# RWKV-7 recurrence and a cosine MoE on one core: the recurrence in units of 64 steps of two batches

## Chip, cores and metric

One core of a Trainium2 chip runs the whole program in one launch. The metric is the device time of that core in microseconds; lower is better. Three runs of the kernel before took 799.08, 800.74 and 801.23 us, median 800.74.

## What is computed

```python
# B, H, S, D = 4, 8, 768, 40; state is (B, H, D, D), zero at the start
for t in range(S):
    y[:, :, t] = np.einsum('bhd,bhde->bhe', rt, state)
    Sa = np.einsum('bhde,bhe->bhd', state, at)
    state_decay = state * wt[:, :, None, :] - np.einsum('bhd,bhe->bhde', Sa, bt)
    state = state_decay + np.einsum('bhd,bhe->bhde', vt, kt)
# x: y as (B*S, H*D) = (3072, 320); w_in (320, 2048) and w_out (2048, 320) are float64
h = x @ w_in
out = (h * np.cos(h)) @ w_out
```

The state of each of the 32 pairs of batch and head is carried through 768 steps. The result of every token goes through the two products of the MoE.

## The kernel before, in words

**The recurrence in chunks.** The 768 steps are 24 chunks of 32 steps, and a chunk holds all four batches: 4*32 = 128 rows of time and batch, eight heads in the free dimension. Within a chunk the recurrence is a triangular system. Its matrix (nps, from a and b scaled by the running product of w) is inverted, and the rest is small products. The chain of a chunk c (the functions `ch_t` to `ch_z`, from line 650) is: `ch_t` transposes the state out of the tile qz, `ch_q` multiplies it by r, `ch_x` makes x0ps from the gram (ag by vvm) and from the state (aT by qz), `ch_s` multiplies by the inverse rt, and `ch_z` makes dps, adds it to the state, and makes the tokens yt. Each ends in PSUM and is copied out by ScalarE or VectorE before the next can start. Chunk c+1 needs the state of chunk c. All these products are 32x32 tiles (72 columns in x, s, z), four batches beside each other.

**What does not need the state** is made ahead: `p1_w`, `p1_a`, `p1_b`, `p1_n` (lines 362 to 476) for two chunks at once, `p2_v`, `p2_k`, `p2_g` (lines 604 to 647) for the next chunk. `p1_w` scales by the running product of w, which `ws_scan` makes ahead for groups of four chunks and which goes through DRAM. The inverse is made by VectorE for four chunks at once: `inv_start`, 31 times `inv_step` (lines 490 to 498), `inv_end`. For the first eight chunks it is made by halves instead (`by_blocks`, lines 512 to 576): 15 steps `pair_step` on the two 16x16 blocks, and TensorE makes the block below by `pair_first` and `pair_second`.

**The MoE** works on 256 tokens at a time (group g, two chunks). For each of four parts j of the hidden width there are four pieces: `first_a` and `first_b` (into ph, with a tail of 64 rows; then the cosine by ScalarE and VectorE in `turns`) and twice `second` (into po). Group 0 has 14 pieces in the list, the others 16 each, and two come at the end. The float64 weights are converted on the chip in 20 items (`rounded`, line 224: VectorE, ScalarE and GpSimd), whose steps `w_steps` are dealt out among the early segments. Tokens go from yt through DRAM (xd) back into xT.

**Order.** It is written out by hand. Every engine works its instructions in the order in which the program issues them. For each chunk a list of segments (lines 1044 to 1102) is issued, where `M` is a place for one MoE piece. `step` issues a segment and then some steps of the inverse (`inv_steps`) and of the weights (`w_steps`). `piece` issues the next piece; `allowed` (line 1041) lets group g in from chunk 2g+2. `later(n, work)` issues work n steps later, above all loads. In the early chunks `busy` and `kept_busy` issue matmuls without use.

**Buffers.** PSUM: `at` (line 324) hands out two tiles of two banks each under one tag; every segment of the recurrence uses it. `ps_h` and `ps_o` hand out two banks each for ph and po. The tags nt, u and inv in SBUF have one buffer each, rt has two.

Two pieces of the order that the text below leans on:

```python
        def allowed(c):
            return done < len(pieces) and 2 * pieces[done][0] + 2 <= c
```
```python
                while seg is s and ("rt", c) not in G:
                    if allowed(c):
                        piece(4, 0)
                    else:
                        inv_steps.pop(0)()
```

## Time and profile before

| | |
|---|---|
| median of three runs | 800.74 us |
| profiled execution, span from the first to the last instruction | 801.4 us |
| TensorE busy | 749.6 us, 94% |
| VectorE, ScalarE, GpSimd busy | 486.7, 387.2, 199.7 us |
| mean granted clock of TensorE | 0.979 |
| MoE matmuls: po, ph with w_in, ph with the tail | 224.5, 186.7, 54.1 us |
| VectorE rows of the full inverse (L494, L498), 4 inverses | 48.2 and 50.6 us |
| matmuls without use (busy) | 23.2 us |

The profiled execution has a span of its own, 0.7 us over the median. In the timeline a row is a run of like instructions: start, length from the first start to the last end, engine, line, operation, tiles, shape, count; in brackets the idle time ahead of it and who ended it. All matmuls stand at line 101 (the helper `mm`), so they are told apart by their tiles: qps, x0ps, sps, dps, gram, nps, sT, below, ph, po. Matmuls are pipelined, so lengths of neighbours overlap, and the distance of two starts says more than a length. PE is TensorE, DVE VectorE, ACT ScalarE, POOL GpSimd, SP the engine that issues most transfers.

### The profile page before, as it was taken

How to read it: one execution, taken by the hardware profiler on the slowest of the kernel's cores; microseconds unless marked ns; L12 is line 12 of the kernel's file. 1: busy time of each engine (PE TensorE's matmuls, PEld its weight loads, DVE VectorE, ACT ScalarE, POOL GpSimd, SP SyncE). 2: the span in 40 equal slices, each digit the busy share in tenths (PEclk: the TensorE clock that was granted, in tenths of full speed). 3: DMA queues.
4: the chain of work that ended last, by engine and by line, in shares of the span. 5: the costliest groups of instructions: out<-in, count | busy, mean ns of one | idle time of the engine just before them, and what ended most of it. 6: DMA issues, size and time to landing. Idle time of an engine off the chain costs nothing.

```text
span 801.4 us, 39602 instructions
## 1 busy us (share of the span) xinstructions
PE 749.6 (94%) x17812; PEld 575.4 (72%) x17812; DVE 486.7 (61%) x1025; ACT 387.2 (48%) x723; POOL 199.7 (25%) x354
## 2 busy tenths in 40 slices
PE   4767899979999999999999999999999999999997
PEld 4634587767777777777777787777787777777775
DVE  8869859744744896553895645994346863323231
ACT  1336667535445436545535635535545445354352
POOL 5316635320321330330330230332031122201000
PEclk9789899999999999999999999999999999999999
DMA  8666572443253314334224314223220222001000
GB/s 111 173 157 157 138 173 66 64 119 66 44 122 68 70 37 67 70 101 69 53 43 65 94 39 71 51 49 71 41 46 21 46 46 57 17 17 33 20 17 16
DMA packets 183304, 55.79 MB, mean 70 GB/s; under 512 B 157152, under 2 KB 178656, under 8 KB 183136
## 3 DMA queue, kind: packets, MB, share of 16 engines
q1 hardware_dynamic: 177440, 52.11, 30.5%
q8 instruction: 140, 2.29, 1.2%
q10 hardware_dynamic: 5440, 0.82, 0.8%
q0 software_dynamic: 256, 0.33, 0.3%
q14 instruction: 28, 0.23, 0.1%
HBM read 42.07 MB, written 11.14 MB: 66 GB/s over the span
## 4 chain that ended last, share of the span: by engine, by line
PE 64%; DVE 18%; ACT 5%; DMA 4%; issue 4%; SPq 3%; POOL 2%; ACTq 0%; DVEq 0%; POOLq 0%
PE ph L101 23%; PE po L101 20%; PE x0ps L101 3%; PE dps L101 3%; DVE inv_tmp L494 3%; DVE rw L395 3%; PE vT L330 2%; DVE inv L498 2%; PE gram L101 2%; SPq L152 2%; PE sps L101 2%; PE nps L101 2%; PE qps L101 2%; DMA nat_a<-in_a_dram 1%; DVE turns L831 1%
## 5 line engine op out<-in xcount | busy, mean ns | idle before, releaser
L101 PE MATMUL po<-w_out_sb,gT 128*128 128x320 f32 x768 | 224.5, 440 | 0.0
L101 PE MATMUL ph<-xT,w_in_sb 128*128 128x256 f32 x768 | 186.7, 388 | 4.4 <-DVE inv_tmp L520 4.4
L101 PEld LDWEIGHTS po<-w_out_sb,gT 128*128 128x128 f32 x768 | 140.6, 190 | 54.2 <-issue 2.0
L101 PEld LDWEIGHTS ph<-xT,w_in_sb 128*128 128x128 f32 x768 | 140.5, 191 | 34.1 <-issue 11.8
L829 ACT ACTIVATE turns<-ph,rnd 128x512 f32<-128x512 f32 x96 | 64.1, 685 | 153.0 <-PE ph L101 152.6
L831 DVE SCALAR_TENSOR_TENSOR turns<-turns,ph 128x512 f32<-128x512 f32 x96 | 64.0, 683 | 114.5 <-ACT turns L829 114.2
L839 DVE TENSOR_TENSOR gT<-ph,turns 128x512 f32<-128x512 f32 x96 | 65.8, 686 | 39.1 <-ACT turns L836 39.1
L755 POOL TENSOR_TENSOR qz<-qz,wc 128x160 f32<-128x160 f32 x92 | 41.9, 475 | 167.2 <-DVE qz L754 166.6
L836 ACT ACTIVATE turns<-turns,half_pi 128x512 f32<-128x512 f32 x96 | 69.3, 722 | 3.1
L835 ACT ACTIVATE turns<-turns 128x512 f32<-128x512 f32 x96 | 60.2, 627 | 18.7 <-DVE turns L831 18.7
L101 PE MATMUL ph<-xT,w_in_tail 64*128 64x256 f32 (+1 forms) x512 | 54.1, 393 | 0.0
L498 DVE TENSOR_TENSOR inv<-inv,inv_tmp 128x31 f32<-128x31 f32 (+15 forms) x124 | 50.6, 408 | 4.3
L586 POOL COPY vp<-nat_v 128x320 f32<-128x320 f32 x24 | 11.9, 494 | 154.3 <-DMA nat_v<-in_v_dram 95.1
L754 DVE TENSOR_TENSOR qz<-dps,qz 128x160 f32<-128x160 f32 x92 | 28.9, 314 | 34.4 <-PE dps L101 34.2
L494 DVE TENSOR_TENSOR inv_tmp<-u,inv 128x31 f32<-128x31 f32 (+15 forms) x124 | 48.2, 389 | 2.3
L395 DVE RECIPROCAL rw<-nat_w 128x320 f32<-128x320 f32 x20 | 42.8, 2142 | 0.1
L658 ACT COPY s<-sT 128x512 f32<-128x512 f32 x46 | 24.5, 584 | 36.5 <-PE sT L654 36.5
L101 PEld LDWEIGHTS ph<-xT,w_in_tail 64*128 64x128 f32 (+1 forms) x512 | 31.8, 160 | 8.9 <-issue 5.3
L766 POOL TENSOR_TENSOR yt<-yt,wb 128x512 f32<-128x512 f32 x24 | 31.6, 1316 | 22.3 <-DVE yt L761 22.3
L718 DVE TENSOR_TENSOR sm<-sps,su 128x128 f32<-128x128 f32 x48 | 11.7, 285 | 32.8 <-ACT sm L713 32.8
L396 POOL TENSOR_TENSOR bn<-nat_b,rw 128x320 f32<-128x320 f32 x22 | 20.1, 912 | 45.1 <-DVE rw L395 36.1
L642 ACT COPY vvm<-gram 128x256 f32<-128x256 f32 x24 | 8.8, 368 | 42.3 <-DVE ag L637 41.9
(136 smaller groups left out, 1123.2 us busy)
## 6 DMA issues: line engine op xcount, KB each, us to landing
words<-in_moe_w_in_dram SPq DMA_DIRECT2D x8, 512.0 KB
xd<-yt SPq DMA_DIRECT2D x48, 80.0 KB
out_dram<-ot SPq DMA_DIRECT2D x24, 160.0 KB
nat_k<-in_k_dram SPq DMA_DIRECT2D x92, 40.0 KB
nat_v<-in_v_dram SPq DMA_DIRECT2D x92, 40.0 KB
nat_r<-in_r_dram SPq DMA_DIRECT2D x92, 40.0 KB
nat_a<-in_a_dram SPq DMA_DIRECT2D x84, 40.0 KB
ws<-in_w_dram SPq DMA_DIRECT2D x5, 640.0 KB
```

The costliest lines, as they stand in the source:

```text
L101: nc.tensor.matmul(o, lhsT=lhsT, rhs=rhs, start=start, stop=stop, skip_group_check=True)
L395: nc.vector.reciprocal(rw, wn)
L494: nc.vector.tensor_tensor(tmp, u[:, j : j + 1, :j].to_broadcast([P, C - j, j]), x[:, j:, j : j + 1].to_broadcast([P, C - j, j]), ALU.mult,)
L498: nc.vector.tensor_tensor(x[:, j:, :j], x[:, j:, :j], tmp, ALU.subtract)
L754: nc.vector.tensor_tensor(z, pick(dp, 0, (2 * N72 + C, 2), (N72, 2), (1, D)), z, ALU.add)
L755: nc.gpsimd.tensor_tensor(z, z, wc.rearrange("p (f m b) -> p f m b", f=2, m=2)[:, :, :, bb] .unsqueeze(3).to_broadcast([P, 2, 2, D]), ALU. ...
L766: nc.gpsimd.tensor_tensor(yt.rearrange("p j b t -> p (j b) t"), yt.rearrange("p j b t -> p (j b) t"), wx, ALU.mult)
L829: nc.scalar.activation(n, u, ACTF.Identity, bias=rnd, scale=1.0)
L831: nc.vector.scalar_tensor_tensor(n, n, -ROUND, u, ALU.add, ALU.subtract)
L835: nc.scalar.activation(n, n, ACTF.Abs)
L836: nc.scalar.activation(n, n, ACTF.Sin, bias=half_pi, scale=-2.0 * math.pi)
L839: nc.vector.tensor_tensor(gT[:, 2 * e : 2 * e + 2].rearrange("p f t -> p (f t)"), us[e], ns[e], ALU.mult)
```

## The change

The unit of the recurrence becomes 64 steps of two batches (C = 64, NB = 2). There are again 24 units: unit u is the step block u//2 of the batch pair u%2, so two chains alternate and each unit follows unit u-2. Products are 64x64 tiles of 104 columns (C + D). The state has two tiles qz, one a chain.

The inverse of a 64x64 triangle is made from its two 32x32 diagonal blocks, as before on VectorE (31 steps for four units; by halves for the first four units alone), and the block beside the diagonal by TensorE: `beside_first` (H0, H1 in the lists) and `beside_second` (R0, R1), each for two units, with GpSimd's `spread` between. `p1_n` also makes the block of the matrix that this needs, and `lower` copies it straight into rt. `ch_x` is split into `ch_ag`, which opens x0ps, and `ch_xa`, which ends it. The lists put s and z of unit u-1 between these two. v and r are loaded in the padded form, so `p2_in` goes; k is loaded by itself; `p2_kn` moves into `ch_z`. The running product of w is joined over two half blocks by `ws_join` with a small transfer. `allowed` lets group g in from unit 2g+3, group 0 at once. `kept_busy`, `shifted` and the blank `dps` matmuls go.

In the lists v, k, g are `p2_*`, t, q, ag, xa, s, z are `ch_*`, pw, pa, pb, pn are `p1_*`, F and S are `pair_first` and `pair_second`; + and - mean the unit after and before.

```diff
-    P, C, DP = 128, 32, 64
+    P, C, DP = 128, 64, 64
+    Q = C // 2
+    HB = Q // 2
+    NB = P // C
...
-    qz = kept("qz", [P, B, 2, NZ], 1, 0.0, on=nc.vector)[0]
...
+    qz = kept("qz", [P, NB, 2, NZ], 2, 0.0, on=nc.vector)
...
+    def ws_join(q):
+        nc.gpsimd.tensor_tensor(ws, ws, we.unsqueeze(1).to_broadcast([P, Q, D]), ALU.mult)
...
         for i in range(2):
             for j in range(4):
-                for bb in range(B):
+                o = (4 * i + j) * Q
+                for bb in range(NB):
                     for e in range(2):
-                        mm(
-                            ps[e][blk[bb ^ e], (4 * i + j) * C : (4 * i + j + 1) * C],
-                            G["bT", c + i][half[e], j, blk[bb]], G["aT", c + i][half[e], j, blk[bb]],
-                            i == 0 and j == 0,
-                        )
-
-        if c % 4 == 0:
-            G["nt"] = sb1.tile([P, C, 4, 2, HH], F32, tag="nt", name="nt")
-            if c < 8:
-                G["noff"] = sb2.tile([P, 4, 2, HH, C], F32, tag="rt", name="noff")
+                        bT, aT = G["bT", u + i][half[e], j], G["aT", u + i][half[e], j]
+                        for m in range(2):
+                            x = slice(C * bb + Q * m, C * bb + Q * m + Q)
+                            to = ps[e][quad[2 * (bb ^ e) + m]]
+                            first = i == 0 and j == 0
+                            if m:
+                                mm(to[:, o : o + Q], bT[:, x], aT[:, x], first)
+                            else:
+                                mm(
+                                    pick(to, o, (8 * Q, 2), (1, Q)), bT[:, x], aT[:, blk[bb]],
+                                    first,
...
+            rt = G["rtq", u // 4]
+            for g in range(NB):
+                for e in range(2):
+                    nc.scalar.copy(
+                        rt[quad[2 * g], u % 4 : u % 4 + 2, HH * e : HH * e + HH, Q:],
+                        ps[e][quad[2 * g], 8 * Q :].rearrange("p (c j t) -> p c j t", c=2, j=HH),
+                    )
...
+    def inv_turn(q):
+        if q:
+            G["rn"] = sb1.tile([P, 4 * H, Q], F32, tag="nt", name="rn")
+        else:
+            G["rn"] = bn_all[:, 5:7].rearrange("p i h d -> p (i h d)").rearrange("p (n s) -> p n s", s=Q)
+        nc.vector.transpose(
+            G["rn"].rearrange("p n s -> p s n"), pick(G["inv"], 0, (1, Q), (Q, Q))
+        )
+
+    def inverse(q):
+        return [
+            inv_start, *(lambda j=j: inv_step(j) for j in range(Q - 1, 0, -1)),
+            lambda: inv_turn(q), lambda: inv_end(q),
+        ]
...
+    def spread(q, p):
+        for g in range(NB):
+            rt = G["rtq", q][quad[2 * g + 1], 2 * p : 2 * p + 2].rearrange("p c h t -> p (c h) t")
+            nc.gpsimd.tensor_copy(rt[:, :, Q:], rt[:, :, :Q])
+            nc.gpsimd.memset(rt[:, :, :Q], 0.0)
+
+    def beside_first(q, p, pool=None):
+        ps = one(pool, "beside")
+        rt = G["rtq", q][:, 2 * p : 2 * p + 2].rearrange("p c h t -> p (c h) t")
+        if q:
+            if not p:
+                G["half"] = sb1.tile([P, 4 * H, Q], F32, tag="u", name="half")
+            h32 = G["half"][:, 2 * H * p : 2 * H * (p + 1)]
+        else:
+            h32 = ring.tile([P, 2 * H, Q], F32, tag="aT", name="half")
+        G["h32", q, p] = h32
+        for n in range(2 * H):
+            for g in range(NB):
+                mm(
+                    ps[quad[2 * g + 1], Q * n : Q * (n + 1)], rt[quad[2 * g], n, Q:],
+                    G["rn"][quad[2 * g], 2 * H * p + n, :], n == 0,
+                )
+        for g in range(NB):
+            rows = quad[2 * g + 1]
+            nc.scalar.copy(h32[rows].rearrange("p n s -> p (n s)"), ps[rows, :])
+        spread(q, p)
...
+    def beside_second(q, p, pool=None):
+        ps = one(pool, "beside")
+        rt = G["rtq", q][:, 2 * p : 2 * p + 2].rearrange("p c h t -> p (c h) t")
+        h32 = G["h32", q, p]
+        for n in range(2 * H):
+            for g in range(NB):
+                rows = quad[2 * g + 1]
+                mm(ps[quad[2 * g], Q * n : Q * (n + 1)], h32[rows, n, :], rt[rows, n, Q:], n == 0)
+        for g in range(NB):
+            rows = quad[2 * g]
+            nc.scalar.copy(rt[rows, :, Q:], ps[rows, :].rearrange("p (n t) -> p n t", t=Q))
+        for i in range(2):
+            G["rt", 4 * q + 2 * p + i] = G["rtq", q][:, 2 * p + i]
...
-    def p2_g(c):
-        kT, vT, aT, rT = G["kT"], G["vT"], G["aT", c], G["rT", c]
+    def p2_g(u):
+        kT, vT, aT, rT = G["kT"], G["vT"], G["aT", u], G["rT", u]
...
+        for x, y, o in ((kT, aT, 0), (vT, rT, HH)):
+            for j in range(4):
+                for bb in range(NB):
+                    for e in range(2):
+                        mm(
+                            ps[blk[bb], e, (o + j) * C : (o + j + 1) * C], x[half[e], j, blk[bb]],
+                            y[half[e], j, blk[bb]], not o and j == 0,
+                        )
...
-        G["ag", c] = ag
...
+        G["ag", u] = ag
...
-        G["s"] = sb1.tile([P, 2 * B, P], F32, tag="s", name="s")
...
+        G["s"] = sb1.tile([P, 2 * NB, P], F32, tag="s", name="s")
+        for i in range(2 * NB):
...
+    def ch_ag(u):
         ps = at("x0ps")
         for j in range(4):
-            o = C * (j // 2)
-            for bb in range(B):
+            for bb in range(NB):
                 for e in range(2):
                     mm(
-                        ps[blk[bb ^ e], e, j * N72 : (j + 1) * N72], G["ag", c][blk[bb], 4 * e + j, :],
-                        vvm[c % 2][blk[bb], 2 * j + e, o : o + N72], j == 0,
+                        ps[blk[bb ^ e], e, j * NW : (j + 1) * NW], G["ag", u][blk[bb], 4 * e + j, :],
+                        vvm[u % 2][blk[bb], 2 * j + e, :], j == 0,
                     )
-        if c:
+        G["x0ps"] = ps
+
+    def ch_xa(u):
+        ps = G["x0ps"]
+        if u > 1:
             for j in range(4):
-                o = (NZ - N72) * (j // 2)
-                for bb in range(B):
+                o = (NZ - NW) * (j // 2)
+                for bb in range(NB):
                     for e in range(2):
                         mm(
-                            ps[blk[bb ^ e], e, j * N72 : (j + 1) * N72],
-                            G["aT", c][half[e], j, blk[bb]], qz[half[e], bb, j % 2, o : o + N72], False,
+                            ps[blk[bb ^ e], e, j * NW : (j + 1) * NW], G["aT", u][half[e], j, blk[bb]],
+                            qz[u % 2][half[e], bb, j % 2, o : o + NW], False,
                         )
-        x0 = [sb1.tile([P, 4 * N72], F32, tag=f"x0{e}", name=f"x0{e}") for e in range(2)]
-        nc.scalar.copy(x0[0], ps[:, 0, : 4 * N72])
-        nc.vector.tensor_copy(x0[1], ps[:, 1, : 4 * N72])
+        x0 = [sb1.tile([P, 4 * NW], F32, tag=f"x0{e}", name=f"x0{e}") for e in range(2)]
+        nc.scalar.copy(x0[0], ps[:, 0, : 4 * NW])
+        nc.vector.tensor_copy(x0[1], ps[:, 1, : 4 * NW])
         G["x0"] = x0
...
-    def ch_z(c):
-        ps = [at("dps") for _ in range(2)]
-        sm = G["sm"]
-
-        wide = c > 3
-        for bb in range(0 if wide else B):
-            for e in range(2):
-                mm(
-                    ps[bb // 2][full[e], bb % 2, : 4 * N72], idle[blk[bb], :DP],
-                    pick(idle[blk[bb]], 0, (0, 4), (1, N72)), True,
-                )
-        for s, n in ((0, kn_b[c % 2]), (1, bn_b[c % 7])):
+    def ch_z(u):
+        ps = at("dps")
+        sm, z_all = G["sm"], qz[u % 2]
+        for s, n in ((0, kn_b[u % 2]), (1, bn_b[u % 7])):
             for j in range(4):
...
-                for bb in range(B):
+                for bb in range(NB):
                     for e in range(2):
-                        first = wide and not s
                         mm(
-                            ps[bb // 2][(full if first else half)[e], bb % 2, j * N72 : (j + 1) * N72],
-                            n[blk[bb], 2 * j + e, : DP if first else D],
-                            sm[e][blk[bb], j, :] if s else vvm[c % 2][blk[bb], 2 * j + e, o : o + N72],
-                            first and j == 0,
+                            ps[(half if s else full)[e], bb, j * NW : (j + 1) * NW],
+                            n[blk[bb], 2 * j + e, : D if s else DP],
+                            sm[e][blk[bb], j, :] if s else vvm[u % 2][blk[bb], 2 * j + e, :],
+                            not s and j == 0,
...
+        if u + 2 < NU:
+            p2_kn(u + 2)
...
-            tails(True)
+            tails(True, full)
             first_full(g, j, 1, False)
         else:
             first_full(g, j, 1)
-            tails(False)
+            tails(False, full if G["ahead"] else [every])
...
-        def allowed(c):
-            return done < len(pieces) and 2 * pieces[done][0] + 2 <= c
...
+        def allowed(u):
+            if done == len(pieces):
+                return False
+            g = pieces[done][0]
+            return not g or 2 * g + 3 <= u
...
+        EARLY = {
+            2: "v k F2 t g F3 S2 q S3 ag H1 v+ xa M R1 k+ M g+ M t+ M",
+            3: "q ag s- M pw4 M pa4 M M z- xa M pb4 v+ M pw6 scan M pn4 pa6 k+ M g+ t+ M",
+            4: "q ag s- M pb6 M pn6 v+ M M z- xa M k+ M pw8 g+ M H0 H1 M R0 t+ M",
+            5: "q ag s- M pa8 M pb8 M M z- xa M pn8 scan v+ M k+ M g+ R1 t+ pw10 M",
+            6: "q ag s- M pa10 M pb10 M M z- xa M pn10 v+ M k+ M g+ t+ M",
+        }
+        STEADY = [
+            "q H0 ag s- M pb M M M z- xa H1 M pn v+ scan M k+ M g+ R0 t+ M",
+            "q ag s- M M M M z- xa M pw v+ M pa k+ M g+ R1 t+ M",
+            "q ag s- M pb M M M z- xa M pn v+ M k+ M g+ t+ M",
+            "q ag s- M M M M z- xa M pw v+ M pa k+ M g+ t+ M",
+        ]
+        LAST = "s- M z- M M M M M M M"
...
+                if name.startswith("H") and u >= 4:
+                    while inv_steps:
+                        if allowed(u):
+                            piece(4, 0)
+                        else:
+                            inv_steps.pop(0)()
```

## The prediction

> **What bounds the kernel now.** I read the table of stretches first, then TensorE's timeline in a steady stretch, then the waits, and last the rows of the engines that release TensorE.
>
> ```profile
> PE 749.6 (94%) x17812; PEld 575.4 (72%) x17812; DVE 486.7 (61%) x1025; ACT 387.2 (48%) x723; POOL 199.7 (25%) x354
> ```
> ```profile
> 40.00:60.00 20.00, 13.16 (x485) 7.87 (x482) 13.38 (x36) 7.85 (x15) 2.61 (x3) 0.83 0.63 156
> 60.00:80.00 20.00, 14.32 (x496) 9.01 (x495) 18.52 (x30) 13.78 (x25) 12.94 (x14) 0.94 0.62 158
> 80.00:100.00 20.00, 16.93 (x463) 11.08 (x462) 17.71 (x33) 13.39 (x25) 13.67 (x15) 0.89 0.51 138
> ...
> 365.00:481.00 116.00, 114.63 (x2784) 89.38 (x2779) 75.86 (x165) 57.29 (x109) 27.00 (x50) 1.00 0.30 60
> ```
> The columns are TensorE (PE), its weight loads, VectorE (DVE), ScalarE (ACT), GpSimd (POOL), clock. From 185 us to the end TensorE has work all the time (114.6 of 116 us in four chunks). There only TensorE time counts. Before that VectorE is the fullest (18.5 of 20 us at 60 to 80), by the conversions of the MoE weights: 58.5 us over their four VectorE rows. So the change has three places: TensorE time per unit, the stretch up to 185 us, and new waits.
>
> ```profile
> 480.25 0.81 PE L101 MATMUL qps<-rT,s 40*40 40x32 f32 x64
> 480.90 1.21 PE L101 MATMUL ph<-xT,w_in_tail 64*64 64x256 f32 x16
> 482.04 1.99 PE L101 MATMUL ph<-xT,w_in_sb 128*128 128x256 f32 x8
> ...
> 488.36 0.88 PE L101 MATMUL x0ps<-vvm,ag 32*32 32x72 f32 x64
> 489.17 0.89 PE L101 MATMUL x0ps<-qz,aT 40*32 40x72 f32 x64
> ...
> 505.61 1.04 PE L654 MATMUL sT<-ident,qz 128*128 128x128 f32 x8
> 506.49 1.89 PE L101 MATMUL ph<-xT,w_in_sb 128*128 128x256 f32 x8
> ```
> Every fp32 matmul of the code stands as two records. I take a group's cost from its start to the next start. The 16 records of 256 columns on four 64x64 tiles take 1.14 us: four rounds of four (a tile's records start 215 ns apart, 0.84 ns a column) and 0.25 us at the edges. So 64x64 tiles do run four abreast.
>
> **Part 1, TensorE per unit.**
> - State: 4 transposes for 8. Eight take 0.88 us, so -0.44.
> - `ch_q`: 32 records of 64 columns, eight rounds of 0.054 and an edge of 0.1: 0.53 for 0.65, so -0.12.
> - The five products (ag, xa, s and two in z): before 64 records, 0.81 each. After, 32 records of 104 columns: eight rounds of 0.088 and an edge, 0.8 each. -0.05 in all.
> - Gram: 1.23 (495.46 to 496.69); after 16 rounds of 0.055 and an edge, 1.0: -0.23.
> - `p1_n`: as many records as before, 9.5 ns each in the trace, 0.
> - The order puts q, ag, s in a row and z, xa in a row: three edges of 0.1 fewer, -0.3.
> - The block beside the diagonal: per four units two firsts and two seconds of 64 records. The nearest row, four 32x32 tiles of 16 columns:
>
> ```profile
> 236.07 0.73 PE L101 MATMUL below<-rt,half 32*32 32x16 f32 x64
> ```
> Its rounds of four start 32 ns apart, though 16 columns stream in 13: the weights set it. The new block has two tiles, so 32 rounds of 0.032 and an edge: 1.1 us each, +1.1 per unit. Bounds: at the records' issue pace (9.5 ns) 0.6; with nothing abreast 2.0.
>
> Sum: -0.44-0.12-0.05-0.23-0.3+1.1 = about 0 per unit. Bounds -0.5 and +0.9 by the block, -10 to +18 us in all. The records' count may set more of this than I allow (rival 2). The Trainium skill, TensorE: Matmul & The Clock Gate, "Back-to-back issue gap", has a floor of about 25 ns between matmul starts however few the columns; by that page 192 records fewer per unit would be 4.8 us a unit. The row of 64 records in 0.81 us, 12.7 ns each, is under that floor, so I don't take it.
>
> **Part 2, new waits of the steady state.** The tag `at` has two PSUM buffers. `ch_ag` now opens x0ps and `ch_xa` closes it after `ch_z`, so one buffer is held from ag to xa, and s must take the one that q used. q's copies:
>
> ```profile
> 540.14 1.17 ACT L670 COPY qz<-qps 40x512 f32<-40x512 f32 x2 [1.00 <-PE qps L101]
> ```
> TensorE began that q at 539.26, so copies end 2.05 us after a q of 0.63, 1.9 after one of 0.47. Between stands only ag, 0.7. So s waits about 0.7 us in each unit, and TensorE's queue with it (the next MoE piece is behind s). Per four units H1 waits 1.0 for z's copies, and two seconds 0.4 each for g's. Together +1.1 per unit, from which the present waits go (1.4 us in 116, 0.35): +0.75. Over 18 units with little else to hide it: +13, of which I keep 11, as q's copies are shorter when ACT is idle. Bounds 0 and 18. The work elsewhere is covered: ACT loses one copy of the state and one of the gram (0.95) and gains the eight of the block and the eight of `lower` per four units (+1.9 per unit) at 57 of 116 us; VectorE changes by +0.1 (larger gram, fewer z); POOL loses 0.96 and gains 1.3 (`spread`) and a join of 3.3 per four units (1316 ns for 512 columns in the yt row), and is at a quarter. The loads keep their packets; w, a, b and k need half the issues on SP. `ws_join` waits on POOL for the small transfer of `ws_scan` (the short transfers of the trace take about 1.9 us), and kn and z stand behind it in POOL's queue; it is emitted two steps later, some 2 to 5 us: 0, bound +2.
>
> **Part 3, up to the first full supply of MoE work.** `allowed` gives group g from unit 2g+3, before from chunk 2g+2; group 0 has 14 pieces. The lists place 4 in u=2 and 9 in u=3, so u=4 has one left. And in u=4 the steps of the second inverse are made from `pn6` on, two a step over six steps; at H0 the other 22 of 34 are emitted at once, with no piece between. Before, that inverse was `by_blocks`, the half-size one, and still cost a wait:
>
> ```profile
> 173.39 3.53 PE L101 MATMUL ph<-xT,w_in_sb 128*128 128x256 f32 x8 [4.44 <-DVE inv_tmp L520]
> ```
> Now it is the full one. A full inverse on VectorE is 98.8/4 = 24.7 us:
>
> ```profile
> L498 DVE TENSOR_TENSOR inv<-inv,inv_tmp 128x31 f32<-128x31 f32 (+15 forms) x124 | 50.6, 408 | 4.3
> ...
> L494 DVE TENSOR_TENSOR inv_tmp<-u,inv 128x31 f32<-128x31 f32 (+15 forms) x124 | 48.2, 389 | 2.3
> ```
> With its transposes (1.25 and 1.9), the copies of nt ahead (1.3) and what the six steps put on VectorE between (z 1.5, x0 0.6, rw 2.15, gram 1.4), H0 starts about 35 us after pn6. TensorE has v, z, xa, k, pw8, g in that time, some 6 us, 9 with their waits. So it stands for about 26 us.
>
> When does pn6 come? Before, nps(6) was at 162.8. VectorE was busy for 93 of the 118 us from 46 (the stretches, the first and last in part); the new order adds 6 to it there (gram, larger transposes, adds), and has less to wait for, since unit 1 doesn't follow unit 0: z of both should end near 63 (before, z1 at 88.8). At full VectorE pn6 would be at 146, at the old share at 171; I take 155, a little nearer to the full end. H0 then at 190. At the same point, pair_first(4), before stood at 185.7, with three pieces more (1.9+3.0+2.3 = 7.2) and without v5, k5, g5 and pw8 (3.6). So after is behind by 4.3+3.6. R0 waits for `spread` (1.5), and after the pause the clock is low: the row at 173.39 shows 3.53 for 1.83 after 4.4 us of idle; 2.5 here. Sum of part 3: 4.3+3.6+4.0 = 12. Bounds by pn6: +3 and +28. The remaining small blocks of before (seven of 0.66) and H0 to R1 (four of 1.1) cancel.
>
> **Part 4, end.** The last unit's outputs go through DRAM (yt, two transfers of 1.9, some 7 us from z); three pieces of group 10 (7.5) cover them: 0, bound +2.
>
> **Sum against the profiled execution** (span 801.4): 0 + 11 + 12 = +23, 824.4. The span is 0.7 over the median of the runs, so 824.
>
> **Rivals.**
> 1. Faster: the two chains win in the early stretch. If VectorE runs full, pn6 is at 146 (-9); if x0ps' hold is covered, -11; if the block goes at issue pace, -10: 792. For it: 35 us of filler matmuls (busy, spare, po and dps from idle) and 42 of idle before 250 (the stretches' sum). Against: VectorE was the fuller engine there, and its work doesn't shrink. All three are needed to get clearly below 801; two land within it. Chance 0.17, and 0.07 for within.
> 2. Faster by far: the number of records sets the time, not their columns. Then half the records cost half: products 5*0.4, q 0.33, gram 0.6, state 0.44, edges 0.3, against +0.6 for the block: -3.1 a unit, 22 units, 756. For it: later records of a group do come at a steady 9.5 to 12.7 ns. Against: in the tails row a tile's own stream of 215 ns sets the rounds, and 104 columns (88 ns) four abreast are slower than that issue. Chance 0.03.
> 3. Slower by far: 64x64 tiles of 104 columns go two abreast. Then five products, q and gram double: 3.5+0.4+0.9 = 4.8 a unit, 915. The tails row speaks against: 0.03.
>
> My own case, the pause in u=4 and the waits for PSUM, has 0.70, and within it pn6 and the waits give 803 to 850. Faster by over 0.3% (about what a measurement of this kernel can tell from no change) 0.20, within 0.07, slower 0.73. The range, 787 to 850, leaves out rival 2 and 3 and the ends.
>
> **What will show it.** Right if TensorE stands 20 us or more ahead of the first `beside` of q=1, on VectorE's inverse; if s waits on ACT's qps copies in each unit; if `beside` takes 1.1 us per 64 records, and the products 0.7 to 0.8. Wrong if pn6 comes well before 150 or after 170, or if the products take 1.4 or 0.4.

## The result, and the profile after

The kernel after takes 926.31 us (median of four runs, 924.73 to 927.34), the kernel before, measured with it, 800.7: ratio 1.1564, 95% interval 1.1545 to 1.1583. The forecast was 824 with a range up to 850. The sign was right; the size was not: +126 us for +23.

The page of the kernel after, busy time and TensorE's granted clock in 40 slices:

```profile
PE 766.8 (83%) x12881; PEld 594.1 (64%) x12881; DVE 515.0 (56%) x968; ACT 413.0 (45%) x761; POOL 195.8 (21%) x309
PEclk9779677985799999999989999899999899999998
```

TensorE is busy for only 17 us more than before (766.8 for 749.6), but the span is 123.2 us longer, 924.6 us. So most of the time, 106 us, is in pauses: 157.8 us without TensorE work, before 51.8. The mean clock fell from 0.979 to 0.916. One of the prediction's stretches (columns: stretch, its length, PE, PEld, DVE, ACT, POOL, clock, DMA share, GB/s), and four units of the later part:

```profile
60.00:80.00 20.00, 15.79 (x399) 10.52 (x398) 6.34 (x14) 6.27 (x13) 7.67 (x10) 0.83 0.13 37
...
390.30:525.40 135.10, 121.58 (x2036) 95.28 (x2036) 77.60 (x150) 62.55 (x116) 26.69 (x43) 0.95 0.27 59
```

Four units take 135.1 us, four chunks before 116. VectorE, the fullest engine of the early stretch before, stands idle for most of 60 to 80 us.

Where the time went is read best from one mark in every unit: the start of `ch_s`, the rows of sps in TensorE's timeline.

| start of s, us | unit 0 | 3 | 4 | 8 | 12 | 16 | 20 | end |
|---|---|---|---|---|---|---|---|---|
| before | 49.9 | 143.0 | 192.1 | 318.4 | 434.7 | 550.9 | 660.8 | 801.4 |
| after | 70.4 | 189.4 | 246.9 | 390.3 | 525.4 | 656.3 | 780.6 | 924.6 |

The marks are read from one profile of each kernel. In the seven profiles of kernels whose first units are issued like those of the kernel after (after, a_moved, a_pace1, a_late, a_late_s, a_noinv4, a_fillpause), s of unit 0 lies between 67.9 and 73.5 us and s of unit 3 between 186.8 and 192.2. So a difference of two or three us at one mark says nothing.

Of the 123.2 us, 46.4 are lost by s of unit 3, 8.4 from there to s of unit 4, 65.0 between units 4 and 20, and 3.4 after that. At s of unit 4 the kernel after has also done four MoE pieces fewer (some 8 us of TensorE), nearly all of which it makes up by unit 20. So the middle part holds some 6 us of moved work and some 59 of loss.

### The profile page after: what moved, and what is told of

Read it like the earlier page. It is cut to its first block, busy times and chain, and to the rows that moved or that the text cites. A ratio compares the mean times of both kernels' runs of the same rounds, so it can differ in the third digit from the quotient of the medians.

```text
span 924.6 us, 29400 instructions
## 1 busy us (share of the span) xinstructions
PE 766.8 (83%) x12881; PEld 594.1 (64%) x12881; DVE 515.0 (56%) x968; ACT 413.0 (45%) x761; POOL 195.8 (21%) x309
## 3 DMA queue, kind: packets, MB, share of 16 engines
q8 instruction: 102, 1.67, 0.7%
## 4 chain that ended last, share of the span: by engine, by line
PE 54%; DVE 23%; ACT 9%; issue 4%; DMA 4%; SPq 2%; POOL 2%; ACTq 0%; POOLq 0%; DVEq 0%
PE ph L75 21%; PE po L75 15%; DVE inv L517 5%; DVE inv_tmp L513 5%; PE dps L75 4%; DVE rw L395 2%; PE sps L75 2%; PE beside L75 2%; ACT qz L721 2%; ACT turns L886 1%; PE gram L75 1%; PE x0ps L75 1%; DVE ag L688 1%; DVE vvm L692 1%; SPq L139 1%
## 5 line engine op out<-in xcount | busy, mean ns | idle before, releaser
L75 PE MATMUL ph<-xT,w_in_sb 128*128 128x256 f32 x768 | 197.1, 403 | 24.3 <-DVE gT L889 24.3
L75 PEld LDWEIGHTS po<-w_out_sb,gT 128*128 128x128 f32 x768 | 143.0, 192 | 53.3 <-issue 3.3
L803 POOL TENSOR_TENSOR qz<-qz,wc 128x160 f32<-128x160 f32 x44 | 20.5, 467 | 378.3 <-DVE qz L802 377.4
L775 DVE TENSOR_TENSOR sm<-sps,su 128x256 f32<-128x256 f32 x48 | 18.1, 419 | 99.7 <-ACT sm L770 99.7
L517 DVE TENSOR_TENSOR inv<-inv,inv_tmp 128x31 f32<-128x31 f32 (+15 forms) x155 | 61.3, 395 | 5.3
L75 PE MATMUL ph<-xT,w_in_tail 64*64 64x256 f32 (+1 forms) x728 | 52.6, 389 | 0.0
L802 DVE TENSOR_TENSOR qz<-dps,qz 128x160 f32<-128x160 f32 x44 | 14.1, 319 | 63.7 <-PE dps L75 63.7
L721 ACT COPY qz<-qps 40x512 f32<-40x512 f32 x44 | 25.4, 578 | 36.0 <-PE qps L75 35.8
L752 ACT COPY x<-x0ps 128x416 f32<-128x416 f32 x24 | 12.1, 505 | 65.8 <-PE x0ps L75 65.8
L75 PE MATMUL sps<-x,rt 64*64 64x104 f32 x768 | 26.0, 276 | 13.6 <-ACT qz L721 11.3
L75 PE MATMUL beside<-rn,rt 32*32 32x32 f32 x640 | 13.2, 200 | 27.4 <-DVE rn L530 23.9
L914 ACT COPY ot<-po 128x320 f32<-128x320 f32 x24 | 10.1, 420 | 56.1 <-DMA out_dram<-ot 45.7
```

Of the source, the lines that this page charges most:

```text
L75: nc.tensor.matmul(o, lhsT=lhsT, rhs=rhs, start=start, stop=stop, skip_group_check=True)
L517: nc.vector.tensor_tensor(x[:, j:, :j], x[:, j:, :j], tmp, ALU.subtract)
L721: nc.scalar.copy(pick(z[rows], 0, (NZ - C, 2), (NZ, 2 * NB), (1, C)), ps[rows, :, : 2 * NB * C].rearrange("p f (i t) -> p f i t", t=C),)
L803: nc.gpsimd.tensor_tensor(z, z, wc.rearrange("p (f m b) -> p f m b", f=2, m=2)[:, :, :, bb] .unsqueeze(3).to_broadcast([P, 2, 2, D]), ALU. ...
```

## Products and blocks: as forecast

TensorE's timeline in a late unit of the kernel after:

```profile
565.71 0.94 PE L75 MATMUL dps<-vvm,kn 64*64 64x104 f32 x32
566.47 0.89 PE L75 MATMUL dps<-sm,bn 64*40 64x104 f32 x32
567.18 0.90 PE L75 MATMUL x0ps<-qz,aT 40*64 40x104 f32 x32
567.90 1.05 PE L75 MATMUL ph<-xT,w_in_tail 64*64 64x256 f32 x16
...
578.01 0.69 PE L75 MATMUL gram<-aT,kT 40*64 40x64 f32 x32
578.52 0.65 PE L75 MATMUL gram<-rT,vT 40*64 40x64 f32 x32
579.10 0.66 PE L705 MATMUL sT<-ident,qz 128*128 128x128 f32 x4
```

From start to start a product takes 0.71 to 0.76 us and the gram 1.09. The 64 records of `beside` take 1.13, to the next start at 623.11:

```profile
621.98 1.20 PE L75 MATMUL beside<-rn,rt 32*32 32x32 f32 x64 [0.22 <-DVE vvm L692]
```

The forecast said 0.8, 1.0 and 1.1. Rival 2 (products of 0.4) and rival 3 (1.4) are refuted by these rows. By the Trainium skill (TensorE: Matmul & The Clock Gate, "Back-to-back issue gap") matmul starts stand at least 25 ns apart; the 64 records of `beside` in 1.13 us are 17.7 ns each, so the measurement again goes below it.

## Experiments on units 4 to 24: the pace of the inverse

The waits of TensorE between 300 and 880 us in the kernel after (engine and what it was to run, whom it waited for, us in total, times, longest):

```profile
PE ph L75 <- DVE gT L889: 17.6, 4, 5.7
PE x0ps L75 <- DVE vvm L692: 7.2, 4, 1.9
PE sT L705 <- DVE vvm L692: 6.0, 8, 1.9
...
PE sps L75 <- ACT qz L721: 5.2, 9, 0.6
```

The first three wait for VectorE, which is busy for 57% of four units. VectorE's and TensorE's timelines at one of the four pauses:

```profile
594.32 0.42 DVE L517 TENSOR_TENSOR inv<-inv,inv_tmp 128x247 f32<-128x247 f32 x1
594.65 1.28 DVE L881 SCALAR_TENSOR_TENSOR turns<-turns,ph 128x512 f32<-128x512 f32 x2
...
597.47 0.68 DVE L889 TENSOR_TENSOR gT<-ph,turns 128x512 f32<-128x512 f32 x1
```
```profile
586.34 1.99 PE L75 MATMUL ph<-xT,w_in_sb 128*128 128x256 f32 x8
588.17 4.47 PE L75 MATMUL po<-w_out_sb,gT 128*128 128x320 f32 x16
598.30 3.75 PE L75 MATMUL ph<-xT,w_in_sb 128*128 128x256 f32 x8 [5.66 <-DVE gT L889]
```

The ph of a piece is full at 588.2 and ScalarE's first step on it ends at 589.1, but VectorE takes its turns up only at 594.65: the inverse's instructions were issued ahead of them and VectorE works in order. Then TensorE has no free ph and stands 5.66 us. The eight records behind the pause take 3.75 us, where the eight at 586.34 take 1.99: the granted clock is 0.50 from 598.3 to 602.0 us.

The reason stands in the one line `fill`, the number of inverse steps and weight steps that `step` issues behind each program step: in the steady part (1, 4) before, (2, 0) after. An average of 57% says nothing of it: while the inverse is issued, VectorE's instructions stand back to back (from 579.8 to 600.2 us without a wait in its timeline). That the pace of issue costs the time is theory A. Theory B says that the units' chain itself costs the time: x0ps holds one of two PSUM buffers, and q, ag and s stand in a row.

**One step instead of two, in the kernel after** (a_pace1), with H0 moved a little later, and the move alone (a_moved):

```diff
-            "q H0 ag s- M pb M M M z- xa H1 M pn v+ scan M k+ M g+ R0 t+ M",
+            "q ag s- M pb M H0 M M z- xa H1 M pn v+ scan M k+ M g+ R0 t+ M",
...
-            fill = (0, 3) if u < 4 else (2, 0)
+            fill = (0, 3) if u < 4 else (2, 0) if u < 6 else (1, 0)
```

> Control for the next run: the kernel after, with H0 of each fourth unit moved from behind q to behind the second piece that follows; the pace of the inverse is untouched, two steps of it per program step. Theory A (from unit 5 on VectorE's queue is filled by two inverse steps per program step, so the first product's cosines come late and TensorE waits): no change beyond 4 us, so 922 to 930 us. Theory B (the loss of the steady units is the chain itself: x0ps holds a PSUM buffer, q, ag and s stand in a row, beside adds TensorE work): H0 no longer waits for copies of q, 2 us less per four units, so 917 to 922.

> The kernel after with H0 as in the control, and from unit 6 on one inverse step per program step instead of two, as the kernel before has it. Theory A: the waits of ph for gT (17.6 us between 300 and 880) go, and with them the low clock behind each (a first product of 3.75 us for 1.83): four units from unit 8 on take some 123 us for 135, four times, so 870 to 890 us. Theory B: within 5 us of the control, since neither the PSUM buffers nor TensorE's work change.

Measured: a_moved 927.81 us (ratio to before 1.1574, 1.1525 to 1.1623), a_pace1 936.03 (1.1663, 1.1611 to 1.1714). The move alone changes nothing, as A said. With one step the waits for gT went, but the kernel was 8 us slower than the control, which neither theory had; A as I had put it failed. TensorE's waits in a_pace1, same stretch up to 860 us, show what came in their place:

```profile
PE beside L75 <- DVE rn L530: 8.7, 4, 2.3
```

With one step a program step not all 34 fit in ahead of H0; the rest is issued there at once, and `beside` waits for it. So the pace can't be taken down unless H0 moves away too. Between s of unit 4 and s of unit 20 TensorE even stands less than in the control (50.0 us for 54.9); it is the work that takes longer, 493 us for 479, at a mean granted clock of 0.90 to 0.96 in the four stretches (control 0.95 to 0.97). A wait of under two us can be enough for that. In the kernel after:

```profile
315.42 1.37 PE L75 MATMUL x0ps<-vvm,ag 64*64 64x104 f32 x32 [1.71 <-DVE vvm L692]
316.50 1.69 PE L75 MATMUL sps<-x,rt 64*64 64x104 f32 x32
```

From 316.4 to 318.4 us the granted clock is 0.50 there, and the 32 records of s take 1.69 us, elsewhere 0.94.

**Two steps instead of one, in the kernel before** (b_pace2), the same pace on untouched chunks:

```diff
+            if c > 5:
+                fill = (2, 4)
             n = len(segs)
```

> The kernel before with the one number changed the other way: from chunk 6 on two inverse steps per program step instead of one. Theory A: it gets waits of ph for VectorE as the kernel after has them, 8 to 13 us in each four chunks with an inverse (four of them), so 825 to 850 us. Theory B: 799 to 805, since its TensorE is full and VectorE is busy for only 75.9 of 116 us.

Measured: 838.92 us, ratio 1.0462 (1.0422 to 1.0502), 37 us more for one number. TensorE's waits between 260 and 800 us:

```profile
PE sps L101 <- DVE x L696: 20.6, 3, 6.9
PE dps L101 <- DVE vvm L643: 5.9, 4, 1.6
```

In the kernel before, these waits are 1.0 us (for x) or absent. The pace alone makes VectorE late, without any 64-step unit. The size is A's; the place is not: the waits are those of s and dps for VectorE, where A had named ph.

**One step, and room for all of them** (a_late): H0, H1, pb and pn stand later in each fourth unit.

```diff
-            "q H0 ag s- M pb M M M z- xa H1 M pn v+ scan M k+ M g+ R0 t+ M",
+            "q ag s- M M M M z- xa M v+ scan H0 M k+ H1 M g+ R0 pb M pn t+",
...
+            fill = (0, 3) if u < 4 else (2, 0) if u < 6 else (1, 0)
```

> One inverse step per program step from unit 6 on, as in the run a_pace1, and the first use of the inverse (H0, H1) moved some twelve program steps later in each fourth unit, with pb and pn behind it, so that all 34 steps are issued before it and none at once. Theory A (VectorE's queue is what costs: two steps a program step fill it, and one a step ends in a burst at H0): waits of ph for gT and of beside for rn both go, four units take 118 to 125 us for 135, in all 880 to 900 us. Theory B (the units' own chain holds the time, as four units took 134 us in a_pace1 too): 920 to 940.

Measured: 901.07 us, ratio 1.1247 (1.1202 to 1.1292), 1 us above what A expected, and far below B's 920. The run changes pace and order together; the late order with two steps was not run. From s of unit 4 to s of unit 20 it takes 510.1 us for 533.7. Waits for gT are gone from the list. Between 384.6 and 511.2 us (units 8 to 12):

```profile
384.60:511.20 126.60, 116.24 (x2032) 91.93 (x2032) 77.85 (x150) 62.63 (x116) 26.98 (x43) 0.99 0.26 55
```

TensorE's own time is 116.2 us for four units, in the kernel before 114.6. What is left against 116 us is 10 us of waits: 3.4 for vvm, 1.7 for q's copies, eight more kinds of 0.4 to 1.2. So the pace, with the order that makes room for it, accounts for some 24 of the 59 us. The other 35 are not priced by any run. Between s of unit 4 and s of unit 20 of a_late TensorE stands 40 us, before 8, in many small waits: 11.5 us for VectorE's vvm, 8.2 for GpSimd's bn, 7.3 of s on q's copies, 3.7 for the copies of `beside`, and smaller ones. B's own wait, the one of s, is among them and not the largest.

**Is the held PSUM buffer one that costs?** (a_late_s) A piece ahead of s in each unit of a_late gives TensorE 2 us while q is copied out (two of the four lists; the other two are changed like the first):

```diff
-            "q ag s- M M M M z- xa M pw v+ M pa k+ M g+ R1 t+ M",
+            "q ag M s- M M M z- xa M pw v+ M pa k+ M g+ R1 t+ M",
-            "q ag s- M pb M M M z- xa M pn v+ M k+ M g+ t+ M",
+            "q ag M s- pb M M M z- xa M pn v+ M k+ M g+ t+ M",
```

> The run a_late with one piece moved ahead of s in each unit from unit 8 on, so that TensorE has 2 us of work between the first half of x0ps and s. Theory E (the PSUM buffer held by x0ps makes s wait for ScalarE's copies of q, 8.4 us in 15 waits between 250 and 860 in a_late): those waits go and the units end earlier, 893 to 897 against 901. Rival (the piece only moves: s is later by its 2 us and what hangs on s waits instead): 899 to 903.

Measured: 907.76 us, ratio 1.1341 (1.1301 to 1.1380), slower than a_late. The waits for qz fell from 8.4 us (250 to 860 us) to 1.2, and another came in (300 to 860 us):

```profile
PE bT L333 <- DVE sm L775: 7.3, 3, 2.4
```

So the wait of s is real, and taking it away in this way gains nothing. But the edit did a second thing: in the list with pb the piece that moved had stood between s and pb. Now pb follows s at once, needs a buffer, and waits 2.4 us for the copies of s, once in each of three units. So the run doesn't price the wait of s alone; that price stays open.

## Experiments on the pause of unit 4

TensorE's timeline there in the kernel after:

```profile
210.87 1.08 PE L75 MATMUL gram<-rT,vT 40*64 40x64 f32 x32
235.81 3.47 PE L75 MATMUL beside<-rn,rt 32*32 32x32 f32 x122 [23.86 <-DVE rn L530]
```

The pause ahead of the first `beside` is 23.86 us (forecast 26), then 122 records take 3.24 us up to the next start, at the later rate (64 in 1.13) 2.2. (The first expectation below sets the row's 3.47 us for 122 records against the 1.13 of 64, and so overstates the low clock there.)

**The second inverse left out** (a_noinv4), **pieces let in** (a_fillpause):

```diff
-            inv_start, *(lambda j=j: inv_step(j) for j in range(Q - 1, 0, -1)),
+            inv_start, *(lambda j=j: inv_step(j) for j in (range(Q - 1, 0, -1) if q > 1 else ())),
```
```diff
-            return not g or 2 * g + 3 <= u
+            return not g or 2 * g + 3 <= u or G.get("early") and g == 1
...
+                G["early"] = u == 4 and name == "H0"
```

> Leaves out the 31 steps (62 instructions on VectorE, 24.7 us) of the second inverse, that of units 4 to 7; its transposes stay. It prices the pause ahead of the first block of unit 4. Theory A: the wait of 23.9 us goes, and the low clock behind it (3.47 us for 1.13, 2.85 for 1.83, and more up to 240 us), so 24 to 30 us less: 896 to 902. Theory B (the pause only hides other late work, such as the loads and the transposes of unit 5, which then show): 10 us less, 914 to 918.

> The kernel after, in which the pieces of the second group of the MoE are let in one unit earlier while the second inverse runs ahead of the first block of unit 4 (some six pieces, 13 us of TensorE work, in a pause of 23.9 us). Theory A (the pause is only missing work): 10 to 16 us less, 910 to 916. Rival: the pieces taken are missing in unit 6, and VectorE, which does the inverse in that pause, must do their cosines too: no gain, 922 to 930.

Measured: a_noinv4 902.02 us (1.1261, 1.1213 to 1.131), 24 less: the pause has the price of its length. a_fillpause 932.64 us (1.1655, 1.1608 to 1.1703), a little slower; the rival holds in kind, 3 us above its range. Its first piece in the pause waits for tokens and its cosines stand on VectorE between the inverse's steps:

```profile
218.95 5.59 PE L75 MATMUL ph<-xT,w_in_sb 128*128 128x256 f32 x16 [6.18 <-DMA xT<-xd]
...
244.64 3.46 PE L75 MATMUL beside<-rn,rt 32*32 32x32 f32 x122 [4.16 <-DVE rn L530]
```

`beside` begins 8.8 us later than without the pieces (244.64 for 235.81). VectorE is the one that is late, so work that needs VectorE was no filler here.

## Experiments on the first 190 us

Eight runs ask why s of unit 3 is 46 us late. The table gives the same mark in each.

| run | median, us | ratio to before, 95% | s of unit 0 | s of unit 3 |
|---|---|---|---|---|
| after | 926.3 | 1.1545 to 1.1583 | 70.4 | 189.4 |
| a_noconv | 916.4 | 1.1410 to 1.1486 | 69.4 | 180.3 |
| a_noW | 903.9 | 1.1247 to 1.1316 | 72.5 | 167.0 |
| a_noblock0 | 915.4 | 1.1371 to 1.1449 | 57.3 | 178.0 |
| a_noM2 | 929.9 | 1.1555 to 1.1634 | 73.5 | 191.5 |
| a_conv3 | 929.6 | 1.1551 to 1.1617 | 72.7 | 192.5 |
| a_kq | 925.6 | 1.1512 to 1.1570 | 68.7 | 187.4 |
| before | 800.7 | | 49.9 | 143.0 |
| b_noconv | 794.7 | 0.9895 to 0.9947 | 49.2 | 134.5 |
| b_noW | 790.6 | 0.9825 to 0.9905 | 47.4 | 128.2 |

**Blocks ahead of the first s.** The kernel before needs one block (F0, S0) ahead of s of chunk 0. The kernel after needs four groups `below`, then two `beside` with `spread` between. TensorE's timeline, `below` in the kernel after:

```profile
50.93 0.78 PE L75 MATMUL below<-bn,noff 32*32 32x16 f32 x70
52.63 0.68 PE L75 MATMUL below<-bn,noff 32*32 32x16 f32 x58 [0.92 <-issue]
...
56.20 0.89 PE L75 MATMUL below<-bn,rt 32*32 32x16 f32 x58 [2.27 <-issue]
...
61.57 1.03 PE L75 MATMUL below<-bn,rt 32*32 32x16 f32 x59 [3.56 <-issue]
```

They take until 62.5, and 6.75 us of that are pauses for which no semaphore is found ("issue"). In a_noblock0 these blocks are not made (the copies and adds that belong to them go too):

```diff
-        step(lambda: pair_first(0, ps_h), 0, 1)
-        step(lambda: pair_first(1, ps_h), 0, 1)
+        step(lambda: None, 0, 1)
+        step(lambda: None, 0, 1)
...
-        step(lambda: beside_first(0, 0, ps_h), 0, 1)
+        step(lambda: spread(0, 0), 0, 1)
```

> Leaves out TensorE's and ScalarE's part of the blocks of units 0 and 1 ahead of the first s (four groups below and two beside); the spread of GpSimd stays. In the kernel after the first s begins at 70.4 us, in the kernel before at 49.9, and between 50.9 and 70 TensorE has those blocks with 6.8 us of idle time that no semaphore explains. Theory F (what stands behind the first z in the queues, the stores of z and the loads of k on SyncE and with them the fetches of the weights' words behind them, comes that much later, and so does all up to unit 4): first s at 53 to 56, s of unit 3 at 172 to 178 for 189.4, total 908 to 914. Theory G (the stretch from 80 to 190 is held by its own order, whenever it starts to be filled): s of unit 3 at 184 to 190, total 921 to 928.

The first s comes 13 us earlier, s of unit 3 11 us, and the end 11 us: what the start loses is never made up. That is F in kind, and each mark comes at the slow end of what F said or a little behind it (57.3 for 53 to 56, 178.0 for 172 to 178, 915.4 for 908 to 914).

**Weights.** In a_noconv the conversion is left out (`taken` and `mantissa` do nothing, `product` is one ScalarE copy of the words), in a_noW the transfers too (`fetch` does nothing, `product` is a memset on GpSimd); b_noconv and b_noW are the same in the kernel before.

> Leaves out the conversion of the MoE weights (seven instructions on VectorE, ScalarE and GpSimd per part of 512 columns); one ScalarE copy of the words stands in its place, and the transfers stay. Theory C (in the first 200 us the conversions stand in the queues of VectorE, ScalarE and GpSimd ahead of the units' copies, and behind the spread and the copies of the new block): s of unit 3, at 189.4 us in the kernel after and 113.9 in the kernel before for chunk 2, 143.0 for chunk 3, comes 50 us earlier, far more than the same cut gives the kernel before. Theory D (the order and the chain of the first units hold them): 20 us earlier, as in the kernel before. Total by C 860 to 885, by D 895 to 915.

> The kernel before with the same conversions left out. VectorE is the fullest engine of its first 185 us, and the conversions are 58.5 us of it, so by C and D alike it gains some 15 to 30 us: 770 to 787. What tells C from D is whether the kernel after gains clearly more than this one.

> Leaves out both the transfers of the MoE weights' words and their conversion; a GpSimd memset stands for each part. Theory H (from 82 to 150 us two paths of about equal length run side by side to the first pieces, the words' transfers through SyncE and the conversions through VectorE and ScalarE, so that cutting one, as a_noconv and a_conv3 did, shows nothing): with both gone s of unit 3 comes at 145 to 160 us for 189.4 and the total is 880 to 895. Theory G (the units' own order holds the stretch: rows of q, ag, H1 and v behind one another on two PSUM buffers): s of unit 3 at 172 to 180, total 908 to 916, little less than a_noconv.

> The kernel before with the same left out: by H and G alike s of its fourth chunk comes at 120 to 134 us for 143.0 and the total is 775 to 794 (b_noconv 794.7). The difference between both kernels at that point, 46 us with the weights' work, is by H some 25 to 30 without it, the blocks of the first units (13 us) among them; by G still 40 to 46.

Without conversions the kernels gain 10 and 7 us: C, by which they hold up the kernel after far more, is refuted, and D's 20 us at s of unit 3 came as 9; both gains are smaller than forecast. With the transfers gone as well, 22 and 10. At s of unit 3 the difference is 38.8 us without the weights' work (167.0 less 128.2) and 46.4 with it. So the weights explain some 8 of the 46 (by one profile each, so give or take some 3), and neither H (25 to 30) nor G (s of unit 3 at 172 to 180) fits whole; G is nearer.

**Order of fetches, of pieces, of the loads of k.** a_conv3 issues weight steps earlier; a_kq moves loads of k to GpSimd's queue; a_noM2 takes the four pieces out of unit 2's list:

```diff
-        step(lambda: pair_second(0, ps_o))
-        step(lambda: pair_second(1, ps_o))
+        step(lambda: pair_second(0, ps_o), 0, 3)
+        step(lambda: pair_second(1, ps_o), 0, 3)
...
-            later(1, lambda: load(u + 1, "k"))
+            later(1, lambda: load(u + 1, "k", nc.gpsimd if u < 5 else nc.sync))
...
-            2: "v k F2 t g F3 S2 q S3 ag H1 v+ xa M R1 k+ M g+ M t+ M",
+            2: "v k F2 t g F3 S2 q S3 ag H1 v+ xa R1 k+ g+ t+",
```

(a_conv3 gives the two `pair_first` three weight steps each as well.)

> Twelve steps of the weights' conversion, the fetches of words among them, are issued along the four groups below of units 0 and 1 instead of two, so ahead of the stores of the first z in SyncE's queue, where the last fetch ahead of a gap of 17 us (63.8 to 80.7) now stands. Theory F: fetches go out in that gap, first piece at 105 to 112 for 122, s of unit 3 at 175 to 180, total 908 to 916. Theory G: 921 to 928.

> The loads of k of the units up to 5 go out from GpSimd's queue instead of SyncE's, where one waits 13.9 us for GpSimd's use of the tile (64.6 to 78) with the fetches of words behind it. If that load alone is what blocks SyncE: as for a_conv3, 908 to 916. If the store of the first z, next in SyncE's queue and ready at 79.9 us, blocks it as well: 923 to 929, with the gap up to 79.9 still there.

> The kernel after with the four MoE pieces of unit 2 taken out of its list; they are issued later, where pieces are let in and one is ready, five of them then in unit 4 while the second inverse runs. Theory D1 (in unit 2 each piece stands in TensorE's queue ahead of s of unit 2 and waits there for its converted weights: s of unit 1 at 75.7 us, first piece at 122, s of unit 2 at 150.3; in the kernel before that gap is 33 us): s of unit 2 comes at 115 to 130, pn6 at 170 to 185, and the pause of 23.9 us gets some 10 us of work; in all 25 to 40 us less, 886 to 901. Theory D2 (the conversions and transfers pace this stretch whatever the order, since the rest of them is forced ahead of pn4): s of unit 3 stays within 5 us of 189 and only the pause gains, 912 to 920.

None of the three made it faster. SyncE's queue does stand in the kernel after, with no fetch of words between 64.6 and 80.7 us:

```profile
63.79 0.80 SPq L236 DMA_DIRECT2D words<-in_moe_w_out_dram  x2
80.74 0.36 SPq L236 DMA_DIRECT2D words<-in_moe_w_in_dram  x1
```

None of the runs took that gap away. In a_kq the loads of k are out of it and the store of the first z stands there until 78.2, as its second case said. a_conv3 issued five more fetches ahead of the gap, but the queue then stood from 66.9 to 80.9 us, and the next fetch of words came at 91.5. Its s of unit 3, 192.5, is like that of the kernel after. So fetching some words earlier didn't help; whether the gap costs is not shown. In a_noM2 the pieces were not the limit: D1 is refuted, and so is its gain in the pause, since `beside` still stood 20.7 us. D2 had the mark right (191.5) and its gain of 6 to 14 us wrong.

**What the rows show between s of unit 1 and s of unit 2.** s of unit 1 is not late (75.7 us, in the kernel before 81.1), s of unit 2 is (150.3 for 113.9). One wait in that stretch can be followed back in the kernel after:

```profile
106.04 0.43 DVE L243 TENSOR_SCALAR conv<-words 128x512 int32<-128x512 int32 x1 [6.22 <-DMA words<-in_moe_w_out_dram]
106.83 0.72 ACT L247 ACTIVATE conv<-conv,to_bits 128x512 int32<-128x512 int32 x1 [6.66 <-DVE conv L244]
108.02 1.15 ACT L721 COPY qz<-qps 40x512 f32<-40x512 f32 x2
109.22 1.07 PE L75 MATMUL beside<-bn,rt 32*32 32x32 f32 x32 [5.17 <-ACT qz L721]
```

VectorE waits for the words of a weight, ScalarE waits for VectorE, q's copies stand behind that conversion in ScalarE's queue, and TensorE waits for the copies. In a_conv3 the same wait for words is 10.2 us and TensorE's 10.5, which fits its gaining nothing; in a_noconv and a_noW TensorE has no such wait ahead of `beside`. So late words hold up the units at this point, by 5 us. What that adds up to is not shown: none of the three runs made the words come in time.

**What stays open.** Of the 46.4 us, 13 are the blocks, about 8 the weights, 5 were late at the first `below` already (50.9 us, before 45.7 at the same point). If these add up, some 20 are left, between s of unit 1 and s of unit 3. Between 100 and 160 us TensorE is busy for 39 us at a mean clock of 0.74, before for 57 at 0.97. I name no cause for the 20: the order of units 2 and 3 is what is left, and no run here rearranged it as a whole.

## Gains together

> The later inverse (a_late, 901.1 us measured) with the earlier fetches of a_conv3. By F the gains add up, as they lie in different stretches: 883 to 891. By G 896 to 903.

> Both edits together on the kernel with the later inverse: pieces of unit 2 taken out, a piece ahead of s, one inverse step per program step. If D1 and E hold and add up: 926.3 less 25 (a_late, measured), less 25 to 40, less 4 to 8, so 855 to 872, still above the kernel before. By D2 and the rival of E: 887 to 897.

a_late_conv took 903.5 us (1.1266, 1.1229 to 1.1302), a_all 908.54 (1.1340, 1.1309 to 1.1371): neither beats a_late, and both are slower than each of their forecasts, as no second edit was worth anything. The best version found, a_late at 901.07 us, is still 12% slower than the kernel before.

## Why the prediction was wrong, step by step

- **Part 1, net 0 per unit: right.** In a_late, where the clock is 0.99, TensorE is busy for 116.2 us in four units, 114.6 before: +0.4 per unit, within the bounds.
- **"VectorE changes by +0.1", called covered: wrong, and the first step that failed.** I counted how long VectorE's instructions last and not how fast they are issued. The lengths were nearly right: VectorE's work grew by 0.4 us a unit (77.60 for 75.86 in four). But `fill` goes from (1, 4) to (2, 0) in the part that I called steady; the whole diff showed it, though the lines printed ahead of the prediction don't include it. The pace alone costs 37 us on the kernel before (b_pace2); taken back together with a later order it gains 25 on the kernel after (a_late). I had used the two steps in Part 3 for unit 4 alone.
- **Part 2, the waits for x0ps' buffer, +11: right in kind, wrong in price.** s waits 0.57 us on ACT's copies (said 0.7), 9 times in 300 to 880 us, not in each unit. Taken away at the cost of another wait, nothing was gained (a_late_s). What the units cost beyond the pace, some 35 us, is spread over a dozen waits of which I had priced three; no run shows their causes.
- **Part 3, the pause of unit 4: right.** 23.86 us for 26, and 24 us by a_noinv4. Its size is partly luck: from pn6 to `beside` it took 41.1 us for 35, and TensorE's work in that time 17.2 for 9; both were too short, and the difference came out.
- **Part 3, pn6 at 155: wrong, the second step that failed.** It came at 194.7 (nps). That is past the 170 that I had named as a sign of being wrong. I worked it out from VectorE's share. VectorE's work up to pn6 was as forecast (95.8 us from 46 us on, for 99), but it was spread over 148.7 us and not 109: from 60 to 80 alone VectorE was idle in 13.7 of 20 us. "z of both should end near 63" left out the four groups `below` and two `beside` that now stand ahead of the first s; z of the two units ended near 77 and 83. That start is worth 11 to 13 us (a_noblock0), the weights some 8; the cause of some 20 stays open.
- **Part 4, end: 3.4 us** from s of unit 20 for 0, bound 2: small, and a little past its bound.
- **Rival 1** would have needed an early stretch with VectorE full; it was further from that than before. Its terms add up to 794 and not 792, and rival 3's, with the 22 units and the 824 that rival 2 takes, to 930 and not 915; neither touches the range.
- **The low clock** I priced once (2.5 us in unit 4). It follows every pause for gT that I looked at, and the mean clock goes from 0.979 to 0.916. After 5.66 us of pause, work of 1.99 us took 3.75. The Trainium skill (TensorE: Matmul & The Clock Gate, "Part 1: The HAM clock gate") has the rate halved after an idle window of about 3.4 us. The trace agrees for that pause, but shows 0.50 after one of 1.71 us too (315.42), so the waits of under 2 us that I counted at their length cost more than that.

## What to carry to other kernels

An engine's mean share tells little of a queue that works in order: read how many instructions per program step are dealt out to it, and compare the busy share in the window in which they are issued. Ahead of the first use in a chain, list every instruction that now must come first; what the start loses was given back nowhere in these runs. And a pause behind a late engine was not filled here by work that needs the same engine.

## What the hardware showed unexpectedly

TensorE's unexplained pauses ("issue") in `below` stand 128 records apart: by the rows of the timeline 127 records lie between the first and the second, and 128 between the second and the third. A record is a matmul with its weight load, so that is 256 instructions. The page counts 102 packets and 1.67 MB in an instruction queue, 16.4 KB a packet; TensorE's 12,881 records with as many weight loads are 100.6 times 256, and in the kernel before its 17,812 are 139.2 times 256, for 140 packets. By the timeline's rows, short matmuls at 9 to 12 ns use up 128 records in about 1.4 us, and the pauses (0.92 to 3.56 us) fall where up to 397 GB/s are moved. That the next packet of instructions is late there is what these numbers suggest; no run here tried it.
